# Attention over a cache on one Trainium2 core: transposed scores, unshifted exp and row sums by a ones-matmul, in place of shifted softmax with transposes of P

## The chip, the cores and the metric

The kernel runs on one core of one Trainium2 chip. The metric is the device time of one execution in microseconds (us). Each kernel is run several times; medians are given with the lowest and the highest run. All times that I compare are of runs with a granted TensorE clock near full speed, unless the text says otherwise.

The engines are called as in the profile: PE (TensorE matmul), PEld (TensorE weight load, which overlaps PE), DVE (VectorE), ACT (ScalarE), POOL (GpSimd) and SP (SyncE, which here issues all loads). "SPq" is SP's sequence of DMA issues.

## The reference, cut to what matters

The program does the same attention block twice, for inputs A and B, and puts the two results side by side.

```python
# B, Sq, D = 16, 144, 448;  H, Sk, Dh = 16, 512, 256;  all inputs bf16
q = (x @ wq).reshape(B, Sq, H, Dh)            # -> b h q d
scores = einsum("bhqd,bhkd->bhqk", q, k_cache) * Dh ** -0.5
p = softmax(scores, axis=-1)
o = einsum("bhqk,bhkd->bhqd", p, v_cache)
out = o.reshape(B, Sq, H * Dh) @ wo           # 448 columns; A and B are concatenated
```

A "unit" in this text is one head of one batch of one input: 2 x 16 x 16 = 512 units. Each needs 256 KB of K and 256 KB of V from memory, so K and V together are 268 MB.

## The kernel before

It is a software pipeline. While unit `i` goes through its last product, later units are at earlier stages. Queries lie on the partitions of the score matrix, so 144 queries need a piece of 112 and a remainder of 32. The remainders of four units are packed into one tile. The maximum of each row is taken (DVE), the exponential is shifted by it and sums its row on the way (ACT), P is normalized (POOL), and P is transposed on PE, because the product with V needs keys on the partitions.

```python
def t_load_k(SG):                              # K: one transposing load of 2 MB for 8 units
    src = ks[pr].rearrange("b h k d -> (b h k) d")[r0 * SK:(r0 + 8) * SK, :]     # 512 B rows
    return q.dma_start_transpose(kt_sb[:, sl, :, :], src)...
def t_load_v(G):                               # V: one plain load of 1 MB for 4 units
    src = vs[pr][b, h0:h0 + 4].rearrange("u (p c) d -> p u (c d)", p=128)
    return q.dma_start(v_sb[:, sl, :, :], src)...
def t_sa(U):                                   # scores of 112 queries, 512 keys wide
    for dc in range(2):
        t.matmul(sa_ps[bank][0:QA, :], lhsT=qt_sb[:, U % NQT, dc, 0:QA],
                 rhs=kt_sb[:, ksl, dc, ko:ko + SK], start=(dc == 0), stop=(dc == 1))
def t_exp(U):
    a.activation(pa_sb[0:QA, psl, :], sa_ps[bank][0:QA, :], AF.Exp,
                 bias=stat[0:QA, NEG + sl:NEG + sl + 1], scale=1.0,
                 accum_out=stat[0:QA, RSUM + sl:RSUM + sl + 1])
# ... t_recip: 1/row sum, 112x1, DVE; t_norm: P times 1/row sum, POOL
def t_ta(U):                                   # transposes of P on PE
    src = pa_sb[0:QA, psl, :].rearrange("q (p c) -> q c p", c=4)
    for c in range(4):
        t.transpose(pta_ps[bank][:, c * 128:c * 128 + QA], src[:, c, :], ident[0:QA, 0:QA])
# ... t_sb, t_exp_b, t_norm_b, t_tb: the same for the remainders of four units at once
def t_pv(U):                                   # O transposed, 8 matmuls of 144 columns
    for dc in range(2):
        for c in range(4):
            t.matmul(ot_ps[ob][:, dc * SQ:(dc + 1) * SQ],
                     lhsT=v_sb[:, vsl, j, c * DH + dc * 128:c * DH + (dc + 1) * 128],
                     rhs=pt_sb[:, sl, c, :], start=(c == 0), stop=(c == 3))
# ... the order of the loads: sorted by the unit that needs them first
for SG in range(NSG):
    dl = 8 * SG - LSB
    lo = 8 * (SG - NK) + 7 - LS + 1 if SG >= NK else s_min
    plan(lo, dl, 12, t_load_k, SG)
for G in range(NG):
    dl = 4 * G
    lo = 4 * (G - NV) + 3 + 1 if G >= NV else s_min
    plan(lo, dl, 8, t_load_v, G)
```

All these loads go through one queue, SP's, in the order of the plan. So the queue carries K, V, V, K, V, V and so on: one transposing load for every two plain ones.

## Time and profile before

| | before |
|---|---|
| time, 3 runs | 1215.06 us (1213.36 to 1216.5) |
| first product with V starts at | 37.9 us |
| from one unit's PV to the next | median 2.01, mean 2.278 us |
| after the last PV | 8.3 us |

The first lines of the profile page of the kernel before: span, then busy time of each engine with its share and number of instructions, then the chain of work that ended last, by engine.

```profile
span 1210.9 us, 33868 instructions
...
PE 1176.6 (97%) x13952; PEld 902.6 (75%) x13952; DVE 770.1 (64%) x2179; ACT 753.9 (62%) x2213; POOL 679.6 (56%) x682
...
PE 90%; DMA 6%; DVE 2%; SPq 1%; ACT 0%; issue 0%; POOL 0%; ACTq 0%
```

PE is the bound: 97% busy, and 90% of the chain. (The mean step is above the median because only some steps carry an output projection.)

Groups of instructions of the kernel before: line, engine, operation, tiles, shapes, count, then total busy us, mean ns of one, and the engine's idle time before them with what ended it.

```profile
L418 PE MATMUL sa_ps<-kt_sb,qt_sb 128*112 128x512 bf16 x1024 | 311.1, 385 | 1.0 <-DVE pt_sb L481 0.8
...
L471 PE MATMUL sa_ps<-ident,pa_sb 112*128 112x112 bf16 x2048 | 186.5, 213 | 0.1
...
L450 DVE RECIPROCAL stat<-stat 112x1 f32<-112x1 f32 x512 | 78.4, 153 | 0.5 <-ACT pa_sb L440 0.5
L342 PE MATMUL sb_ps<-kt_sb,qt_sb 128*32 128x512 bf16 x1024 | 67.9, 385 | 10.5 <-DMA kt_sb<-in_A_k_cache_dram 7.9 <-DMA kt_sb<-in_B_k_cache_dram 0.8 <-issue 0.6
```

The change removes the first, the second and the last of these from PE. The third is a reciprocal of one column, 153 ns; the trace has none of more than one column (that of the remainders, 128x1, also takes 153 ns). The mean of one matmul holds its latency; what a matmul costs PE is the distance to the next, which I read from the timeline.

### The profile page before, as it was taken

What the parts mean: (1) busy time and instruction counts of PE and PEld (TensorE: products, weight loads), DVE (VectorE), ACT (ScalarE), POOL (GpSimd) and SP (SyncE); (2) the same over time, 40 slices, a digit from 0 to 9 for tenths busy, and PEclk for the clock granted to TensorE, in tenths of its full rate; (3) what the DMA queues carried; (4) which work ended last, traced back from release to release, by engine and by line L of the source; (5) the groups of instructions that cost most, each with busy time, mean ns of one, the idle gap of its engine ahead of it and who ended that gap; (6) DMA issues with size and microseconds to landing.
All of it is one profiled execution on the core that took longest, in us unless ns stands there. A gap on an engine that the chain in (4) does not pass through costs nothing.

```text
span 1210.9 us, 33868 instructions
## 1 busy us (share of the span) xinstructions
PE 1176.6 (97%) x13952; PEld 902.6 (75%) x13952; DVE 770.1 (64%) x2179; ACT 753.9 (62%) x2213; POOL 679.6 (56%) x682
## 2 busy tenths in 40 slices
PE   4998999999999999999999999999999999999997
PEld 3676777777777777777777777777877777777765
DVE  1765666666666666666566666666666666666563
ACT  1655666666666666666566666666666666666553
POOL 0654565565555565565555655655655655655553
PEclk9999999999999999999999999999999999999999
DMA  9999999999999999999999999999999999999971
GB/s 250 296 269 290 246 255 225 242 251 246 245 238 234 228 263 231 239 239 233 278 284 272 278 272 267 247 257 224 245 245 236 226 245 244 244 239 243 223 178 47
DMA packets 627033, 294.15 MB, mean 243 GB/s; under 512 B 548416, under 2 KB 556608, under 8 KB 626880
## 3 DMA queue, kind: packets, MB, share of 16 engines
q1 hardware_dynamic: 625152, 287.85, 102.2%
q0 software_dynamic: 1728, 4.13, 1.2%
q8 instruction: 111, 1.82, 0.6%
q14 instruction: 42, 0.34, 0.1%
HBM read 148.90 MB, written 4.13 MB: 126 GB/s over the span
## 4 chain that ended last, share of the span: by engine, by line
PE 90%; DMA 6%; DVE 2%; SPq 1%; ACT 0%; issue 0%; POOL 0%; ACTq 0%
PE qp_ps L314 20%; PE ot_ps L504 19%; PE sa_ps L418 18%; PE op_ps L542 17%; PE sa_ps L471 8%; PE sb_ps L342 5%; DMA kt_sb<-in_A_k_cache_dram 4%; PE sb_ps L394 2%; DMA kt_sb<-in_B_k_cache_dram 1%; DVE stat L429 1%; DMA wq_sb<-in_A_wq_dram 0%; PE qp_ps L542 0%; SPq L280 0%; DVE qt_sb L326 0%; DVE pt_sb L481 0%
## 5 line engine op out<-in xcount | busy, mean ns | idle before, releaser
L458 POOL TENSOR_TENSOR pa_sb<-pa_sb,stat 112x512 bf16<-112x512 bf16 x512 | 532.7, 1041 | 491.6 <-DVE stat L450 491.4
L440 ACT ACTIVATE pa_sb<-sa_ps,stat 112x512 bf16<-112x512 f32 x512 | 352.0, 688 | 409.6 <-DVE stat L429 408.6
L429 DVE TENSOR_REDUCE stat<-sa_ps 112x1 f32<-112x512 f32 x512 | 353.9, 691 | 324.7 <-PE sa_ps L418 321.4
L314 PEld LDWEIGHTS qp_ps<-xt_sb,wq_sb 128*128 128x128 bf16 x4096 | 290.5, 99 | 93.1 <-issue 11.3
L314 PE MATMUL qp_ps<-xt_sb,wq_sb 128*128 128x144 bf16 x4096 | 344.1, 228 | 16.1 <-DMA wq_sb<-in_A_wq_dram 10.3
L504 PE MATMUL ot_ps<-pt_sb,v_sb 128*128 128x144 bf16 x4096 | 340.9, 226 | 0.0
L418 PE MATMUL sa_ps<-kt_sb,qt_sb 128*112 128x512 bf16 x1024 | 311.1, 385 | 1.0 <-DVE pt_sb L481 0.8
L542 PE MATMUL op_ps<-wo_sb,ring 128*128 128x448 bf16 x1120 | 279.6, 353 | 0.0
L504 PEld LDWEIGHTS ot_ps<-pt_sb,v_sb 128*128 128x128 bf16 x4096 | 269.1, 98 | 0.4
L471 PEld LDWEIGHTS sa_ps<-ident,pa_sb 112*128 112x128 bf16 x2048 | 161.2, 114 | 104.9 <-ACT pa_sb L440 24.8
L519 ACT ACTIVATE ring<-ot_ps 128x288 bf16<-128x288 f32 (+8 forms) x512 | 190.3, 372 | 4.5 <-PE ot_ps L504 4.5
L481 DVE COPY pt_sb<-sa_ps 128x448 bf16<-128x448 bf16 x512 | 190.5, 372 | 2.4 <-PE sa_ps L471 2.4
L471 PE MATMUL sa_ps<-ident,pa_sb 112*128 112x112 bf16 x2048 | 186.5, 213 | 0.1
L326 DVE TENSOR_SCALAR qt_sb<-qp_ps 128x288 bf16<-128x288 f32 x256 | 117.0, 457 | 98.2 <-PE qp_ps L314 97.5
L382 POOL TENSOR_TENSOR pb_sb<-pb_sb,stat 128x512 bf16<-128x512 bf16 x128 | 133.1, 1040 | 27.1 <-DVE stat L374 27.1
L330 ACT ACTIVATE qt_sb<-qp_ps 128x288 bf16<-128x288 f32 x256 | 106.0, 414 | 35.1 <-PE qp_ps L314 33.4
L418 PEld LDWEIGHTS sa_ps<-kt_sb,qt_sb 128*112 128x112 bf16 x1024 | 96.9, 129 | 38.5 <-issue 26.8
L542 PEld LDWEIGHTS op_ps<-wo_sb,ring 128*128 128x128 bf16 x1120 | 95.5, 98 | 28.1 <-issue 0.9
L440 ACT ACTIVATION_READ_ACCUMULATOR pa_sb<-sa_ps,stat 112x1 f32 x512 | 98.9, 193 | 0.0
L354 DVE TENSOR_REDUCE stat<-sb_ps 128x1 f32<-128x512 f32 x128 | 87.1, 680 | 3.6 <-PE sb_ps L342 3.6
L364 ACT ACTIVATE pb_sb<-sb_ps,stat 128x512 bf16<-128x512 f32 x128 | 88.5, 691 | 0.0
L450 DVE RECIPROCAL stat<-stat 112x1 f32<-112x1 f32 x512 | 78.4, 153 | 0.5 <-ACT pa_sb L440 0.5
(23 smaller groups left out, 368.4 us busy)
## 6 DMA issues: line engine op xcount, KB each, us to landing
v_sb<-in_A_v_cache_dram SPq DMA_DIRECT2D x64, 1024.0 KB, 6.0
v_sb<-in_B_v_cache_dram SPq DMA_DIRECT2D x64, 1024.0 KB, 6.1
out_dram<-ost_sb POOLq DMA_DIRECT2D x36, 112.0 KB, 5.1
wo_sb<-in_A_wo_dram SPq DMA_DIRECT2D x8, 448.0 KB, 7.4
wo_sb<-in_B_wo_dram SPq DMA_DIRECT2D x8, 448.0 KB, 5.7
wq_sb<-in_A_wq_dram SPq DMA_DIRECT2D x4, 768.0 KB, 6.2
wq_sb<-in_B_wq_dram SPq DMA_DIRECT2D x4, 768.0 KB, 7.8
wq_sb<-in_A_wq_dram SPq DMA_DIRECT2D x4, 128.0 KB, 6.6
```

Of the source, the lines that this page charges most:

```text
L314: ins = t.matmul(qp_ps[:, dc * SQ:(dc + 1) * SQ], lhsT=wq_sb[:, kc, c0:c0 + 128], rhs=xt_sb[:, xsl, kc, xo:xo + SQ], start=(kc == 0 and dc ...
L326: return v.tensor_scalar(qt_sb[:, sl, :, :], src, 1.0 / 16.0, None, op0=ALU.mult)
L382: return g.tensor_tensor(pb_sb[:, psl, :], pb_sb[:, psl, :], stat[:, RINVB + sl:RINVB + sl + 1].to_broadcast([128, SK]), op=ALU.mult)
L418: ins = t.matmul(sa_ps[bank][0:QA, :], lhsT=qt_sb[:, U % NQT, dc, 0:QA], rhs=kt_sb[:, ksl, dc, ko:ko + SK], start=(dc == 0), stop=(dc == 1))
L429: return v.tensor_reduce(stat[0:QA, NEG + sl:NEG + sl + 1], sa_ps[bank][0:QA, :], axis=AX.X, op=ALU.max, negate=True)
L440: return a.activation(pa_sb[0:QA, psl, :], sa_ps[bank][0:QA, :], AF.Exp, bias=stat[0:QA, NEG + sl:NEG + sl + 1], scale=1.0, accum_out=stat ...
L458: return g.tensor_tensor(pa_sb[0:QA, psl, :], pa_sb[0:QA, psl, :], stat[0:QA, RINV + sl:RINV + sl + 1].to_broadcast([QA, SK]), op=ALU.mult)
L471: ins = t.transpose(pta_ps[bank][:, c * 128:c * 128 + QA], src[:, c, :], ident[0:QA, 0:QA])
L481: return v.tensor_copy(pt_sb[:, sl, :, 0:QA], pta_ps[bank][:, 0:512].rearrange("p (c q) -> p c q", c=4)[:, :, 0:QA])
L504: ins = t.matmul(ot_ps[ob][:, dc * SQ:(dc + 1) * SQ], lhsT=v_sb[:, vsl, j, c * DH + dc * 128:c * DH + (dc + 1) * 128], rhs=pt_sb[:, sl, c, ...
L519: ins = a.activation(ring[:, 2 * h:2 * h + 2, c0:c0 + n1], src[:, :, 0:n1], AF.Copy)
L542: ins = t.matmul(acc[0:m, 0:D], lhsT=ring[:, c, col0:col0 + m], rhs=wo_sb[:, c, :], start=(c == first), stop=(c == last))
```

## The change

The intent is to take work off PE. With keys on the partitions of the scores (K as weights, Q as moving data) the scores come out already transposed, for all 144 queries at once, so the transposes of P and the whole remainder path go away. Rows of P then lie across partitions, so the maximum and the row sum are no longer cheap on DVE and ACT. The maximum is dropped (exp unshifted, with a check that the sums stayed within 2 to the power of plus or minus 40, else the old kernel runs as a fallback inside the same program). The row sums come from PE: POOL adds the four key chunks in fp32, and one ones-matmul in float32r sums over the partitions and hands every partition the result. The reciprocal is taken of a full 128x144 tile, and the normalization moves to the eviction of O. K is read as rows of 2 KB (four keys) instead of 512 B, so that the scores' key order fits that of V.

The core of the diff, put in order of the functions, with cuts marked; the copy of the old kernel as the fallback, about two thirds of it, is left out.

```diff
-    LQ, LS, LT = 15, 5, 2
-    NK, NV, NXG = 3, 3, 3
+    LQ, LS = 15, 2
+    NK, NV, NXG = 5, 4, 3
 ...
-    kt_sb = sb("kt_sb", [128, NK, 2, 8 * SK], BF16)
+    kt_sb = sb("kt_sb", [128, NK, 8, UG * 128], BF16)        # UG = 4 heads
+    ones = sb("ones", [128, 128], F32R)
+    ps_sb = sb("ps_sb", [128, NPS, SQ], F32R)
 ...
     def t_load_k(G):
-        src = ks[pr].rearrange("b h k d -> (b h k) d")[r0 * SK:(r0 + 8) * SK, :]
+        src = ks[pr].rearrange("b h (p c) d -> (b h p) (c d)", c=4)[r0 * 128:(r0 + UG) * 128, :]
         return q.dma_start_transpose(kt_sb[:, sl, :, :], src)...
 ...
+    def t_s(U):                       # 8 matmuls of 144 columns
+        for c in range(4):
+            for dc in range(2):
+                t.matmul(s_ps[bank][:, c // 2, (c % 2) * SQ:(c % 2 + 1) * SQ],
+                         lhsT=kt_sb[:, ksl, 2 * c + dc, jj * 128:(jj + 1) * 128],
+                         rhs=qt_sb[:, U % NQT, dc, :], start=(dc == 0), stop=(dc == 1))
+    def t_presum(U):                  # POOL
+        g.tensor_tensor(pp_sb[:, sl, :, :], pt_sb[:, psl, 0:2, :], pt_sb[:, psl, 2:4, :], op=ALU.add)
+        g.tensor_tensor(ps_sb[:, sl, :], pp_sb[:, sl, 0, :], pp_sb[:, sl, 1, :], op=ALU.add)
+    def t_sum(U):                     # PE
+        t.matmul(ot_ps[ob][:, 2 * SQ:3 * SQ], lhsT=ones[:, :], rhs=ps_sb[:, sl, :], start=True, stop=True)
+    def t_recip(U):                   # DVE, 128x144
+        v.reciprocal(rinv_sb[:, sl, :], ot_ps[ob][:, 2 * SQ:3 * SQ])
+    def t_check(U):                   # DVE, twice per unit
+        for k, op in ((0, ALU.max), (1, ALU.min)):
+            v.tensor_tensor(run_sb[:, k, :], run_sb[:, k, :], rinv_sb[:, sl, :], op=op)
 ...
-        for SG in range(NSG):
-            dl = 8 * SG - LSB
-            plan(lo, dl, 12, t_load_k, SG)
+        for G in range(NG):
+            dl = UG * G - LS
+            lo = UG * (G - NK) + UG - 1 - LS + 1 if G >= NK else s_min
+            plan(lo, dl, 20, t_load_k, G)
```

## The prediction

> **What bounds it now.** TensorE. Busy shares (part 1): PE 97%, DVE 64%, ACT 62%, POOL 56%; the chain that ended last is 90% PE, 6% DMA. In the timeline around 600 us the PE is back to back: Q 0.50 us per unit (8 matmuls, 62 ns apart), scores 0.44, transposes of P 0.19, PV 0.51, output projection 0.185 per matmul (0.405 per unit), 32-row remainder 0.13 and its transposes 0.055. Sum 2.23 us x 512 units = 1142 us (K loads repeat every 18.0 us per 8 units: 2.25). The rest is start (first PV at 37.9 us), tail (8 us after the last PV) and early waits for K (waits view: 8.7 us).
>
> DMA is second. It looks 90% busy, but by packets it has slack: K transposes run at 290 GB/s (18 ns per 256 B packet), V at 390 to 400; 7.3 us for 2 MB of K plus 2 x 2.7 us for V plus 1.5 to 2.5 us of switching is about 15 us of the 18. Estimated DMA floor: 970 us.
>
> **What changes on PE, per unit.** Out: scores 0.44, remainder scores 0.13, transposes 0.19 + 0.055 = 0.82 us. In: 8 score matmuls of 128x144, like PV, 0.51 us; one float32r ones-matmul, x. So T = 0.50 + 0.51 + 0.51 + 0.405 + x = 1.92 + x, against 2.23. The trace has no float32r matmul. The Trainium skill, "FP8 and Floating Point Precision", TensorE Precision Notes, describes reduced-precision FP32 as one 4-byte read truncated, against four passes for true FP32. One pass is 0.06 us; I add about 0.11 us for a weight load that is not hidden: x = 0.17, possible 0.06 to 0.40. T = 2.09 us. All of it is critical.
>
> **Other engines, per unit (estimates from this trace).** ACT: exp over 576 columns about 0.70, Q eviction 0.41: 1.15 us. POOL: 288- and 144-element adds at 1041 ns per 512: about 0.9 us (now 1.3). DVE: reciprocal of 144 columns about 0.31 (one per column plus the 0.153 us of one element), scaled eviction of 288 columns 0.46, two running max/min about 0.25 each: 1.3 us. None exceeds T. Exp and adds take about 2 us of the 4 before the sum needs them.
>
> K from 2 KB rows moves the same bytes in the same 256 B pieces; I expect it neutral, within 10% of 290 GB/s. The check costs 2 to 4 us at the end.
>
> **Sum.** 512 x 2.09 = 1070, + start and tail about 42, + 5 of stalls and check: about **1118 us**, 8% less. Range 1058 to 1215. Chances: faster 0.80, same 0.10, slower 0.10.
>
> **Signs.** Right: PE still over 93% of the span and of the chain; the score, Q and PV groups 62 to 64 ns apart; sum matmul adding 0.1 to 0.25 us to the step; POOL and DVE below 75%; eight-unit period near 16.7 us.
>
> **What would make it wrong.** (1) The skill's "VectorE: DVE Perf Modes" (slices) gives reciprocal a repeat count of 8; one element here (0.153 us) can't tell. At 8 cycles per column it costs about 1.36 us, DVE then needs 2.3 to 2.5 us per unit and bounds the kernel at 1190 to 1290. (2) Slower K transposes from 2 KB strides, or more switching stalls: PE waits on K. (3) DVE and POOL slowing each other.

## More of the kernel before

The DMA queue of the kernel before in its middle, from the timeline of SP: start, length until the next issue is possible, instruction.

```profile
432.98 3.72 SPq L299 DMA_DIRECT2D v_sb<-in_A_v_cache_dram  x2
436.75 12.05 SPq L290 DMA_TRANSPOSE kt_sb<-in_A_k_cache_dram  x1
448.85 5.66 SPq L299 DMA_DIRECT2D v_sb<-in_A_v_cache_dram  x2
454.55 13.43 SPq L290 DMA_TRANSPOSE kt_sb<-in_A_k_cache_dram  x1
```

And what the queue itself waited for in the kernel before, in total us, times, longest:

```profile
SPq L299 <- PE op_ps L542: 235.3, 59, 12.8
SPq L299 <- PE ot_ps L504: 40.1, 15, 8.0
```

The queue waits some 275 us for PE to free the buffers of V. So the DMA is faster than the kernel needs, but not by 275 us: during most of these waits an earlier load is still on its way. By the landings in the trace, this queue was without a load in flight for only about 16 us before its last landing at 1185 us.

## The result, and the profile after

| | before | after |
|---|---|---|
| time, 4 runs each, same rounds | 1214.21 us (1212.06 to 1216.5) | 1172.11 us (1169.79 to 1177.78) |
| ratio of fast runs, 95% interval | | 0.9662 (0.9632 to 0.9691) |
| first PV starts at | 37.9 us | 36.9 us |
| PV to PV, median / mean | 2.01 / 2.278 us | 2.01 / 2.198 us |
| after the last PV | 8.3 us | 15.3 us |

Ratios in this text are the mean time of one kernel's fast runs over the mean of the other's of the same rounds, so they are not quite the ratio of the medians quoted. The change gained 42 us, against the 96 us that were forecast. The time lies inside the forecast range, but less than half of the gain came.

The same three lines of the page, after:

```profile
span 1176.0 us, 32740 instructions
...
PE 1087.5 (92%) x13952; PEld 961.7 (82%) x13952; DVE 1009.5 (86%) x2184; ACT 560.1 (48%) x1061; POOL 645.1 (55%) x1065
...
PE 64%; DMA 21%; DVE 8%; SPq 4%; issue 1%; ACT 1%; POOL 0%; POOLq 0%; ACTq 0%
```

PE is busy 89 us less (1176.6 to 1087.5); the forecast was 72 (512 x 0.14). But its share of the chain fell from 90% to 64%, and DMA with SPq has 25%, DVE 8%. Two new limits have taken part of the gain.

Groups after:

```profile
L1035 DVE RECIPROCAL rinv_sb<-ot_ps 128x144 f32<-128x144 f32 x512 | 540.4, 1055 | 136.5 <-PE ot_ps L1025 129.5
L988 POOL TENSOR_TENSOR pp_sb<-pt_sb 128x288 f32<-128x288 bf16 x512 | 374.9, 732 | 474.5 <-ACT pt_sb L979 472.4
...
L967 PE MATMUL s_ps<-qt_sb,kt_sb 128*128 128x144 bf16 x4096 | 343.1, 227 | 33.9 <-DMA kt_sb<-in_A_k_cache_dram 18.6 <-DMA kt_sb<-in_B_k_cache_dram 15.1
...
L1063 DVE TENSOR_TENSOR run_sb<-run_sb,rinv_sb 128x144 f32<-128x144 f32 x1024 | 276.6, 311 | 0.0
...
L1025 PE MATMUL ot_ps<-ps_sb,ones 128*128 128x144 f32 x512 | 161.1, 315 | 0.0
L1025 PEld LDWEIGHTS ot_ps<-ps_sb,ones 128*128 128x128 f32 x512 | 98.2, 192 | 0.0
```

The reciprocal takes 1055 ns, not the 310 of the prediction. The two check operations take 311 ns each. The ones-matmul needs a weight load of 192 ns, where a bf16 weight load takes 98. On the score line, PE sits idle 33.9 us in total until K lands.

What PE waited for after, in us, times, longest (the DMA lines of the view of waits):

```profile
PE s_ps L967 <- DMA kt_sb<-in_A_k_cache_dram: 18.6, 19, 2.4
PE s_ps L967 <- DMA kt_sb<-in_B_k_cache_dram: 15.1, 11, 3.4
...
PE qp_ps L939 <- DMA wq_sb<-in_B_wq_dram: 6.6, 3, 4.9
...
PE qp_ps L939 <- DMA xt_sb<-in_A_x_dram: 4.0, 2, 2.1
PE op_ps L1098 <- DMA wo_sb<-in_B_wo_dram: 3.8, 2, 3.5
...
PE ot_ps L1013 <- DMA v_sb<-in_A_v_cache_dram: 1.9, 3, 0.8
```

With 1.5 us more for x of the second input, these sum to 51.5 us. Before, everything but the first load was 8.7 us, shown above on L342. It isn't only K: whatever comes through that queue is late.

The queue after, in the same window as before:

```profile
437.12 0.58 SPq L924 DMA_DIRECT2D v_sb<-in_A_v_cache_dram  x1
437.75 6.84 SPq L915 DMA_TRANSPOSE kt_sb<-in_A_k_cache_dram  x1
444.63 0.58 SPq L924 DMA_DIRECT2D v_sb<-in_A_v_cache_dram  x1
445.26 7.15 SPq L915 DMA_TRANSPOSE kt_sb<-in_A_k_cache_dram  x1
452.45 0.58 SPq L924 DMA_DIRECT2D v_sb<-in_A_v_cache_dram  x1
```

And the largest waits of V's issues for PE:

```profile
SPq L924 <- PE qp_ps L939: 17.0, 39, 1.1
SPq L924 <- PE s_ps L967: 16.6, 27, 1.5
```

Before, the queue waited 235 us and 40 us for a free V buffer in its two largest lines. Now the largest are 17 us each, none longer than 1.5 us. All waits of V's issues for PE are 59 us now, in 117 pieces, and K and V alternate without a pause in the window shown. By the landings in the trace, the queue had a load in flight all the time from its first issue to its last landing at 1146.5 us, with gaps of under 1 us in all. The DMA's slack is gone, and it is the DMA that sets the pace over long stretches. What the queue moved is on the page: packets, MB, and the time of the packets as a share of 16 engines' span (packets overlap, so it can exceed 100%).

```profile
q1 hardware_dynamic: 627200, 287.86, 109.1%
```

K and V are 268 MB of it. The other 19 MB are x and the weights, which go through the same queue.

The waits cost a little more than their length. This is PE's timeline after the longest wait for K: start, us, instructions, and in brackets the idle time before.

```profile
600.27 0.68 PE L967 MATMUL s_ps<-qt_sb,kt_sb 128*128 128x144 bf16 x8 [3.45 <-DMA kt_sb<-in_B_k_cache_dram]
...
601.59 1.18 PE L939 MATMUL qp_ps<-xt_sb,wq_sb 128*128 128x144 bf16 x8
...
604.66 0.67 PE L939 MATMUL qp_ps<-xt_sb,wq_sb 128*128 128x144 bf16 x8
```

After 3.45 us of idleness the eight Q matmuls that start 1.3 us later take 1.18 us, and the next eight, at 604.66, 0.67 again. The Trainium skill, "TensorE: Matmul & The Clock Gate", What's actually happening, says that the clock halves after an idle window of about 3.4 us and comes back after about the same time of work; here the trace's record of the clock agrees: it is halved from 601.18 to 604.60 us. Less idleness was enough elsewhere: the clock is halved at 720.65 us after an idle stretch of 2.1 us, and in the kernel before at 586.74 us after one of 2.0 us. All slowed matmuls together cost about 7 us by my count (outside start and end the clock was halved for 27 us), and the mean granted clock fell from 0.997 to 0.985.

### The profile page after: what moved, and what is told of

Its sections match the earlier page's. It is cut to its first block, busy times and chain, and to the rows that moved or that the text cites. A ratio compares the mean times of both kernels' runs of the same rounds, so it can differ in the third digit from the quotient of the medians.

```text
span 1176.0 us, 32740 instructions
## 1 busy us (share of the span) xinstructions
PE 1087.5 (92%) x13952; PEld 961.7 (82%) x13952; DVE 1009.5 (86%) x2184; ACT 560.1 (48%) x1061; POOL 645.1 (55%) x1065
## 4 chain that ended last, share of the span: by engine, by line
PE 64%; DMA 21%; DVE 8%; SPq 4%; issue 1%; ACT 1%; POOL 0%; POOLq 0%; ACTq 0%
PE qp_ps L939 16%; PE s_ps L967 15%; PE ot_ps L1013 15%; PE op_ps L1098 15%; DMA kt_sb<-in_B_k_cache_dram 9%; DMA kt_sb<-in_A_k_cache_dram 8%; DVE rinv_sb L1035 4%; PE ot_ps L1025 3%; SPq L905 2%; DVE run_sb L1063 2%; DVE ring L1050 2%; DMA v_sb<-in_A_v_cache_dram 1%; DMA xt_sb<-in_A_x_dram 1%; SPq L915 1%; SPq L906 1%; DMA wq_sb<-in_A_wq_dram 1%
## 5 line engine op out<-in xcount | busy, mean ns | idle before, releaser
L1035 DVE RECIPROCAL rinv_sb<-ot_ps 128x144 f32<-128x144 f32 x512 | 540.4, 1055 | 136.5 <-PE ot_ps L1025 129.5
L988 POOL TENSOR_TENSOR pp_sb<-pt_sb 128x288 f32<-128x288 bf16 x512 | 374.9, 732 | 474.5 <-ACT pt_sb L979 472.4
L955 ACT ACTIVATE qt_sb<-qp_ps 128x288 bf16<-128x288 f32 x512 | 210.0, 410 | 470.4 <-PE qp_ps L939 470.3
L979 ACT ACTIVATE pt_sb<-s_ps 128x576 bf16<-128x576 f32 x512 | 332.9, 650 | 108.9 <-PE s_ps L967 67.8
L967 PE MATMUL s_ps<-qt_sb,kt_sb 128*128 128x144 bf16 x4096 | 343.1, 227 | 33.9 <-DMA kt_sb<-in_A_k_cache_dram 18.6
L967 PEld LDWEIGHTS s_ps<-qt_sb,kt_sb 128*128 128x128 bf16 x4096 | 275.4, 98 | 42.6 <-DMA kt_sb<-in_A_k_cache_dram 22.5
L1063 DVE TENSOR_TENSOR run_sb<-run_sb,rinv_sb 128x144 f32<-128x144 f32 x1024 | 276.6, 311 | 0.0
L992 POOL TENSOR_TENSOR ps_sb<-pp_sb 128x144 fp32r<-128x144 f32 x512 | 251.7, 492 | 40.1
L1050 DVE TENSOR_TENSOR ring<-ot_ps,rinv_sb 128x288 bf16<-128x288 f32 (+8 forms) x640 | 242.4, 395 | 17.7
L1025 PE MATMUL ot_ps<-ps_sb,ones 128*128 128x144 f32 x512 | 161.1, 315 | 0.0
```

The source lines that it names most:

```text
L955: return a.activation(qt_sb[:, sl, :, :], src, AF.Copy)
L967: ins = t.matmul(s_ps[bank][:, c // 2, (c % 2) * SQ:(c % 2 + 1) * SQ], lhsT=kt_sb[:, ksl, 2 * c + dc, jj * 128:(jj + 1) * 128], rhs=qt_sb[ ...
L979: return a.activation(pt_sb[:, psl, :, :].rearrange("p (a b) q -> p a (b q)", a=2), s_ps[bank][:, :, 0:2 * SQ], AF.Exp, scale=DH ** -0.5)
L988: return g.tensor_tensor(pp_sb[:, sl, :, :], pt_sb[:, psl, 0:2, :], pt_sb[:, psl, 2:4, :], op=ALU.add)
L992: return g.tensor_tensor(ps_sb[:, sl, :], pp_sb[:, sl, 0, :], pp_sb[:, sl, 1, :], op=ALU.add)
L1025: return t.matmul(ot_ps[ob][:, 2 * SQ:3 * SQ], lhsT=ones[:, :], rhs=ps_sb[:, sl, :], start=True, stop=True)
```

## The experiments

I held two theories of where the missing 54 us (1172 less 1118) went, and a third way of reading the first:

- **Supply.** The DMA can't bring K and V as fast as PE now uses them. My first version of it (A1 where the texts say so) blamed the number of switches between K and V in the queue: K and V alternate one to one now, where before there was one K for two V. Another version blames the 2 KB rows, and a third the number of transposing loads.
- **DVE.** The reciprocal is slower than forecast; DVE, 86% busy, holds buffers that PE needs.
- **PE itself.** The steps of the prediction's sum, above all the ones-matmul, may have been too small.

Every kernel of one batch ran on one chip beside the kernel before (medians of that: 1212.7 to 1214.2).

### Taking DVE's and the DMA's load away: nocheck, halfk, halfk_nocheck

`nocheck` drops the two check operations of each unit (only the reduction at the end stays, over an untouched tile).

```diff
                 t_evac_ot(u)
-                t_check(u)
```

> After, without the running max/min of the reciprocals per unit (DVE falls from 1.97 to about 1.43 us per unit; result still right, but unguarded). Theory A, the supply of K through the DMA queue bounds the kernel: 1155 to 1175 us, no gain beyond 1.5%. Theory B, DVE at 1.97 us per unit bounds it: 1095 to 1120 us.

`halfk` loads K only for every second group of four units, and the group between uses its neighbour's. It computes a wrong thing; it shows the kernel with half of the K traffic. `halfk_nocheck` does both.

```diff
-            ksl = G % NK
+            ksl = (G - G % 2) % NK
 ...
-            plan(lo, dl, 20, t_load_k, G)
+            if G % 2 == 0:
+                plan(lo, dl, 20, t_load_k, G)
```

> After, loading only every second K group and using it twice (wrong result on purpose): a quarter of the DMA bytes gone, every instruction of PE, DVE, ACT and POOL kept. Theory A: 1085 to 1115 us, PE over 95% busy, no waits for K. Theory B (DVE): 1150 to 1175 us.

> Both at once (wrong result on purpose): what PE alone allows. Dense step from the trace of after: 24 matmuls at 63 ns, 0.119 us for the sum, 0.405 us of output projection = 2.04 us x 512 + 42 = about 1087 us. Theory A: within 1.5% of halfk. Theory B: far below halfk.

| kernel | us, 4 runs | ratio to before |
|---|---|---|
| after | 1172.11 (1169.79 to 1177.78) | 0.966 |
| nocheck | 1162.29 (1159.23 to 1169.11) | 0.9565 (0.9536 to 0.9594) |
| halfk | 1110.79 (1110.52 to 1112.39) | 0.9154 (0.9133 to 0.9174) |
| halfk_nocheck | 1094.82 (1094.68 to 1095.33) | 0.9019 (0.900 to 0.9038) |

The busy lines of `halfk`, then of `halfk_nocheck`:

```profile
PE 1071.7 (97%) x13952; PEld 954.4 (86%) x13952; DVE 1006.5 (91%) x2184; ACT 560.0 (51%) x1061; POOL 645.2 (58%) x1065
```

```profile
PE 1063.8 (97%) x13952; PEld 954.7 (87%) x13952; DVE 786.6 (72%) x1160; ACT 560.0 (51%) x1061; POOL 641.7 (59%) x1065
```

This divides the time. With both loads lightened PE is 97% busy at 1095 us, and no DMA wait but the first one is left in `halfk`. Putting the check back costs 16 us (1110.8 less 1094.8). Putting the other half of K back costs 61 us more (1172.1 less 1110.8). Of those 61, the waits listed above are 51.5 and the slowed matmuls about 7. So the main loss is supply, the smaller one DVE, and PE alone does what the prediction's sum says, as shown further down. (`halfk` also has half of K's loads and half of the changes between K and V in the queue, so it shows that supply costs 61 us, not what in the supply does.)

A caution that holds for all K edits here: `halfk` was compared with the reference and found correct, though half of its K is wrong. The comparison passes with these inputs, so "correct" is weak evidence that a K layout is right. For `kold` and `k8` below I have only the agreement of the indices in the code besides.

### Is it the rows, or the order in the queue? kold and pair

`kold` reads K from 512 B rows as the kernel before did, in the same groups of four units, with a strided weight access to match.

```diff
-            src = ks[pr].rearrange("b h (p c) d -> (b h p) (c d)", c=4)[r0 * 128:(r0 + UG) * 128, :]
+            src = ks[pr].rearrange("b h k d -> (b h k) d")[r0 * SK:(r0 + UG) * SK, :]
 ...
-                                       lhsT=kt_sb[:, ksl, 2 * c + dc, jj * 128:(jj + 1) * 128],
+                                       lhsT=kt_sb[:, ksl, dc, jj * SK:(jj + 1) * SK].rearrange("d (p c) -> d c p", c=4)[:, c, :],
```

> After, with K transposed from 512 B rows as in the kernel before (1 MB loads kept; the weights of the score matmuls are then read with a stride of 4). Theory A1, the switches between transposes and plain loads cost, not the row size: 1160 to 1185 us, K packets at the same 18 ns. Theory A2, the 2 KB rows slow the transposes: 1150 us or less. Theory A3, the 2 KB rows help them: 1195 us or more.

It took 1176.67 us (1168.63 to 1185.03), ratio 0.9687 (0.9624 to 0.9749), the same as after. The times from issue to landing of K's loads, by the view of that line, are also the same; first after, then `kold`:

```profile
DMA to landing us min/median/max: 7.1/10.6/15.1
```

```profile
DMA to landing us min/median/max: 6.9/10.7/14.6
```

In both, and in the kernel before, K moves at about 290 GB/s while it moves alone, and a packet of 256 B takes 18 ns. The Trainium skill, "DMA: Bandwidth & Descriptors", Latency and other measured facts, gives 261 GB/s for transposing loads with a non-contiguous middle dimension and 350 to 400 for contiguous ones; this case shows 290 for 512 B and for 2 KB rows alike. The prediction's "neutral" was right about rows.

`pair` keeps everything but the order: K, K, V, V instead of K, V, K, V.

```diff
-            dl = UG * G - LS
-            lo = UG * (G - NK) + UG - 1 - LS + 1 if G >= NK else s_min
+            dl = UG * (G - G % 2) - LS
+            G1 = G - G % 2 + 1
+            lo = UG * (G1 - NK) + UG - 1 - LS + 1 if G1 >= NK else s_min
 ...  # and V likewise
```

> After, with the loads issued two K groups, then two V groups, instead of one and one: same bytes, same buffers, half as many switches between transposes and plain loads. Theory A with about 1 us lost per switch (249 us lost in 238 switches of the trace of after): 1100 to 1140 us. Theory B (DVE): no change, 1165 to 1180 us. If the deeper wait for two free buffers costs more than the switches: slower than 1180.

It took 1142.72 us (1137.93 to 1148.59), ratio 0.9428 (0.9392 to 0.9465): 29 us gained with the same loads, and PE waits no more for K. Its largest wait for K or V in `pair` is now one for V:

```profile
PE ot_ps L1013 <- DMA v_sb<-in_B_v_cache_dram: 6.6, 2, 3.3
```

At this point I took the switches between K and V for the cause.

### The ladder on top of pair: pair_x_v5, pair_x_v5_pck, pair_x_v5_pck_bf, pair_pck

I tried to build on that. `pair_x_v5` adds a fifth V buffer (one x buffer less) and loads x 16 units earlier. `pck` moves half of the check to POOL: a running sum of the reciprocals in place of their maximum (a sum of positive numbers is at least their maximum, so the check stays safe). `bf` makes the ones and the partial sums bf16, so that the ones-matmul is a bf16 one. `pair_pck` is `pair` with that check alone. (The two `pair_x_v5` kernels with `pck` also get a third buffer for the reciprocals, `pair_pck` doesn't.)

```diff
-    NK, NV, NXG = 5, 4, 3
+    NK, NV, NXG = 5, 5, 2
 ...
-            dl = u_first - LQ
+            dl = u_first - LQ - (16 if XG else 0)
 ...  # pck
-            for k, op in ((0, ALU.max), (1, ALU.min)):
+            for k, op in ((0, ALU.add), (1, ALU.min)):
-                S.add(DVE, e, ...
+                S.add(DVE if k else POOL, e, ...
 ...  # bf
-        ones = sb("ones", [128, 128], F32R)
+        ones = sb("ones", [128, 128], BF16)
-        ps_sb = sb("ps_sb", [128, NPS, SQ], F32R)
+        ps_sb = sb("ps_sb", [128, NPS, SQ], BF16)
```

> The paired order, with five V groups instead of four (room from one x buffer less) and x asked for 16 units earlier. The trace of pair has four waits of 3 to 4 us for V and x and about 6 us of matmuls at the lower clock after them: without them 1115 to 1128 us. If what is left in pair is something else (DVE, raw DMA rate): 1138 us or more.

> The same, with the upper half of the check as a running sum on GpSimd (one add of 144, about 0.49 us, instead of a running max on DVE). DVE falls from 1.97 to 1.71 us per unit, GpSimd rises from 1.26 to 1.75. halfk against halfk_nocheck says that DVE is worth at most 16 us: 1100 to 1118 us.

> The same, with the presums written in bf16 and a bf16 ones-matmul in place of float32r. The sum adds 0.119 us to the step of PE in the trace of after; at bf16 it should add 0.063: 0.056 x 512 = 29 us less if PE bounds, 1072 to 1092 us. If DMA or DVE bounds by then: less than 10 us gained.

> The paired order with the upper half of the check as a sum on GpSimd, nothing else: the plain candidate for a better kernel. 1130 to 1143 us: DVE relief is worth 0 to 12 us beside DMA.

| kernel | us | ratio to before |
|---|---|---|
| pair | 1142.72 (1137.93 to 1148.59) | 0.9428 |
| pair_pck | 1142.97 (1141.58 to 1145.81) | 0.9413 |
| pair_x_v5 | 1141.61 (1139.65 to 1144.96) | 0.9404 |
| pair_x_v5_pck | 1138.65 (1136.81 to 1140.57) | 0.9385 |
| pair_x_v5_pck_bf | 1135.87 (1130.83 to 1141.97) | 0.9343 |

All of it together gains 7 us; the gains expected of `pair_x_v5` and of `pck`, 24 us and more, didn't come. In the last of these PE still waits 32 us for V, where `pair` had 9. Work taken from PE and DVE comes back as waiting, as it must where the DMA sets the pace. The bf16 step did shorten PE's own step: the ones-matmul adds 62 ns instead of 119, and the median step falls from 2.009 to 1.941 us.

### Switches, or transposing loads? split_same and split_alt

`split_same` cuts each load of K into two of two heads, issued back to back. The number of switches between K and V doesn't change; the number of transposing loads of K doubles to 256. `split_alt` cuts V as well and alternates the halves, so that both double.

```diff
-        def t_load_k(G):
+        def t_load_k(G, part):
-            src = ...[r0 * 128:(r0 + UG) * 128, :]
+            r1 = (r0 + 2 * part) * 128
+            src = ...[r1:r1 + 256, :]
 ...
-            plan(lo, dl, 20, t_load_k, G)
+            for part in range(2):
+                plan(lo, dl, 20, t_load_k, G, part)              # split_same
+                plan(lo, dl + 2 * part, 20 + 2 * part, t_load_k, G, part)   # split_alt, and V likewise
```

> After, each 1 MB load of K as two transposes of 2 heads issued one behind the other, V unchanged: twice the transposes, the same 256 switches. Theory A1 (the switch costs): 1165 to 1185 us. Rival A5 (each transpose instruction or smaller piece costs): 128 more at about 0.65 us each, 1225 to 1265 us.

> After, K in halves and V in halves, taking turns (K V K V per group of 4 heads): twice the switches, about 512. The traces put a switch at about 0.65 us of lost DMA time: if DMA bounds, up to 166 us more, 1260 to 1340 us under A1. If the gain of pair came from anything but the number of switches: within 2% of after.

`split_same` took 1268.67 us (1260.22 to 1271.87), ratio 1.0464 (1.044 to 1.0487). `split_alt` took 1261.12 us (1258.45 to 1268.34), ratio 1.0396 (1.0353 to 1.044). The largest DMA waits of PE in `split_same`, then in `split_alt`, where the deadlines of the halves shift the waiting from K to V:

```profile
PE s_ps L969 <- DMA kt_sb<-in_A_k_cache_dram: 54.1, 42, 2.9
...
PE s_ps L969 <- DMA kt_sb<-in_B_k_cache_dram: 43.8, 40, 3.9
```

```profile
PE ot_ps L1017 <- DMA v_sb<-in_A_v_cache_dram: 60.5, 27, 8.8
...
PE ot_ps L1017 <- DMA v_sb<-in_B_v_cache_dram: 38.9, 24, 4.0
```

The switches can't be the only cost. Without one switch more, the time rose by 96 us, slightly above what A5 expected and far above A1; with twice the switches, it rose no further (its 1261 us lie just inside A1's range, but A1 can't explain `split_same`). So cutting K's loads in two costs by itself: (1268.7 less 1172.1) / 128 = 0.755 us for each transposing load added, in a queue that is the bottleneck. `pair` stands against the opposite reading, that switches cost nothing: it gained 29 us with the same loads.

### Fewer transposing loads: k8

`k8` undoes the part of the change that the prediction didn't price: it loads K for eight units at a time, as the kernel before, but keeps the 2 KB rows. Two more things change with it. The order of the queue becomes K, V, V again, with half of the switches, as in `pair`. And three such buffers replace five small ones (24 units of K instead of 20), and x, Q and the output get fewer buffers so that all fits; no run tests these alone.

```diff
-    NK, NV, NXG = 5, 4, 3
+    NK, NV, NXG = 3, 4, 2
-        kt_sb = sb("kt_sb", [128, NK, 8, UG * 128], BF16)
+        kt_sb = sb("kt_sb", [128, NK, 8, 8 * 128], BF16)
 ...
-            src = ...[r0 * 128:(r0 + UG) * 128, :]
+            src = ...[r0 * 128:(r0 + 8) * 128, :]
-        for G in range(NG):
-            dl = UG * G - LS
+        for G in range(NT // 8):
+            dl = 8 * G - LS
```

> After, with K loaded as one 2 MB transpose per 8 heads (three such buffers; room from one x buffer, three Q slots and one output slot), V unchanged, result right: 64 transposes of K instead of 128. Theory A5 (each transpose instruction costs about 0.75 us of DMA time, from split_same): 48 us less DMA need, so the kernel comes near the floor of halfk (1111): 1112 to 1132 us, waits for K under 15 us. Theory A1 (switches only): like pair, 1135 to 1145.

It took 1126.5 us (1124.51 to 1129.66), ratio 0.9283 (0.926 to 0.9305): 46 us less than after and 16 less than `pair`, inside A5's range and below A1's. The K waits of PE and the queue in `k8`:

```profile
PE s_ps L967 <- DMA kt_sb<-in_B_k_cache_dram: 5.1, 3, 2.7
...
PE s_ps L967 <- DMA kt_sb<-in_A_k_cache_dram: 3.8, 2, 2.1
```

```profile
439.21 14.91 SPq L915 DMA_TRANSPOSE kt_sb<-in_A_k_cache_dram  x1
454.17 1.12 SPq L924 DMA_DIRECT2D v_sb<-in_A_v_cache_dram  x2
455.34 15.46 SPq L915 DMA_TRANSPOSE kt_sb<-in_A_k_cache_dram  x1
```

PE waits 8.9 us for K instead of 33.7; before the change it was 8.7. So the halving of K's loads, with the order of the queue that comes with it, costs 46 us. That is 0.71 us for each of the 64 loads, close to the 0.755 of `split_same`, but the two can't be set side by side: `k8` also has half of the switches of after, and being only 16 us above `halfk` it is in part bound by PE and DVE.

The landings in the traces show the queue itself. The queue time below counts each load from the later of its issue and the landing before it, to its own landing, summed over all loads of the profiled run. In all five kernels a load was in flight up to the last landing, with gaps of under 1 us in all.

| kernel | order for eight units | transposing loads of K | switches, about | queue time, us | that run, us |
|---|---|---|---|---|---|
| k8 | K V V | 64 | 128 | 1083 | 1125.8 |
| pair | K K V V | 128 | 128 | 1097 | 1137.9 |
| after | K V K V | 128 | 256 | 1146 | 1177.8 |
| split_same | K K V K K V | 256 | 256 | 1238 | 1263.3 |
| split_alt | K V K V K V K V | 256 | 512 | 1233 | 1260.7 |

From `k8` to `pair`, 64 more loads at equal switches add 13 us; from `pair` to after, 128 more switches at equal loads add 49; from after to `split_same`, 128 more loads at equal switches add 92; doubling both adds 87. No single price for a load, or for a switch, gives all four. What is shown is that the same bytes cost more in smaller pieces and in an order that alternates.

### Other suspects: wide, vact, vact_bf, vact_pck_bf

The traces also hold 111 instruction fetches of 16 KB, each about 1.05 us long on one DMA engine. In stretches with K alone, all engines' transposes lose about 1.5 us around one (mean of 24 cases after, 30 before, by my own reading of the packets). `wide` has fewer instructions: Q, scores and PV as 4 matmuls of 288 columns each instead of 8 of 144. Its result is wrong (relative error 0.95).

```diff
-                    for dc in range(2):
-                        ins = t.matmul(qp_ps[:, dc * SQ:(dc + 1) * SQ], ...
+                    ins = t.matmul(qp_ps[:, 0:2 * SQ], lhsT=wq_sb[:, kc, h * DH:h * DH + 128],
+                                   rhs=xt_sb[:, xsl, kc, x2:x2 + 2 * SQ], ...
 ...  # scores and PV likewise
```

> After, with Q, scores and PV as 4 matmuls of 288 columns in place of 8 of 144 (wrong result on purpose, same columns, same DMA issues, 12,288 fewer instructions of PE). In the traces the 16 KB instruction fetches cost the K transposes about 1.5 us each (111 of them). Theory A4, these stalls are a large part of what DMA loses: fetches fall to about 63, PE's step by only 0.03 us, time 1090 to 1125 us. If fetches don't matter (only switches do): 1155 to 1172.

It took 1148.56 us (1138.78 to 1151.32), ratio 0.9434 (0.939 to 0.9478), and missed what both theories expected. The queue line of instruction fetches (packets, MB, share), after and then in `wide`:

```profile
q8 instruction: 111, 1.82, 0.6%
```

```profile
q8 instruction: 63, 1.03, 0.4%
```

Of 48 fetches less, 24 us came. Half a microsecond each would fit, but PE's median step also fell, by 0.08 us and not by the 0.03 expected (2.010 to 1.931; 40 us over 512 units if PE alone bounded), so the fetches' share stays open. They can't explain the difference between before and after, which have 111 each.

`vact` issues the loads of V from ACT, on a second queue beside K.

```diff
-            S.add(SP, e, writes=[(("v", sl), G)], dma_sem="v%d" % sl, name="v%d" % G)
+            S.add(ACT, e, writes=[(("v", sl), G)], dma_sem="v%d" % sl, name="v%d" % G)
 ...
-            lo = UG * (G - NV) + UG - 1 + 1 if G >= NV else s_min
+            lo = UG * (G - NV) + UG - 1 + 3 if G >= NV else s_min
```

> After, with the V loads issued from ACT (their own queue, 3 units after the buffer is free at the soonest), everything else as in after, result right. If switching within one queue and V standing behind K is what costs: V and K mix, 1105 to 1135 us. If the DMA engines themselves are full: 1160 to 1180 us. If ACT is held up by its waits: slower than 1180.

> vact with the bf16 presum and ones-matmul. If DMA no longer bounds vact, up to 29 us less than vact where PE bounds, about 10 to 15 where DVE (1.97 us per unit) does; if DMA still bounds, within 5 us of vact.

> The same with half of the check on GpSimd as a sum (DVE 1.71 us per unit). If PE bounds: step 1.98 us, 1065 to 1085 us. If DMA bounds: within 5 us of vact_bf.

`vact` took 1281.46 to 1288.93 us in its three fast runs (a fourth, of 1348.05, was slow), ratio of the fast runs 1.0587 (1.0548 to 1.0625): worse by some 112 us, and uneven. `vact_bf` ran from 1260.79 to 1440.27 us, with two of four runs slow and no ratio; `vact_pck_bf`, which also has a third buffer for the reciprocals, took 1271.23 to 1282.91 us in three fast runs, ratio 1.0498 (1.0464 to 1.0533), and up to 1339.79 in three slow ones. Its profile fell in a slow run, so I read nothing from it. The landing times of K in `vact`, to set against those of after shown above:

```profile
DMA to landing us min/median/max: 6.9/12.8/43.6
```

A load of K now needed up to 43.6 us, and PE waited 124 us for K. In a stretch from about 450 to 610 us all DMA together moved only 104 to 168 GB/s. One expectation for more than 1180 us was that ACT would be held up by its waits; but PE waited only 7.9 us for V, which ACT issues, so what was late is K. Here the waits between the two kinds of load in one queue are cheaper than mixing them; why K slows down so much isn't shown.

### Putting it together: k8_pck_bf and k8_bf

`k8_pck_bf` is `k8` with half of the check on POOL and the bf16 ones-matmul; `k8_bf` leaves the check on DVE.

> The same with the bf16 sum and half of the check on GpSimd. If DMA is off the critical path in k8: PE's step 1.98 and DVE at 1.71 us, 1075 to 1100 us. If DMA still bounds: within 8 us of k8.

> k8 with the bf16 sum alone, the check left on DVE. In the trace of k8_pck_bf the one check left on DVE took 521 ns where two took 2 x 311 in after, so moving the other to GpSimd freed almost nothing: 1110 to 1120 us, within 6 us of k8_pck_bf. If moving it did help: 1122 us or more.

`k8_pck_bf` took 1115.58 us (1113.14 to 1117.81), ratio 0.9181 (0.9164 to 0.9197): the fastest of all whose result was found right, 8% faster than the kernel before and 5% faster than after. I had expected 1075 to 1100. `k8_bf` took 1119.82 us (1117.27 to 1125.51), ratio 0.9239 (0.9204 to 0.9275), 4 us more. By these medians the bf16 sum gives 7 us and the moved check 4, by the ratios about 5 and 7; for the sum alone the intervals of the ratios overlap. Clear of the noise are only the two together, 11 us. That `k8_bf` stayed below 1122 fits the expectation that moving the check freed little. The check's two halves in `k8_pck_bf`, in the groups:

```profile
L1063 DVE TENSOR_TENSOR run_sb<-run_sb,rinv_sb 128x144 f32<-128x144 f32 x512 | 267.0, 521 | 0.0
L1063 POOL TENSOR_TENSOR run_sb<-run_sb,rinv_sb 128x144 f32<-128x144 f32 x512 | 257.3, 502 | 5.1 <-DVE rinv_sb L1035 5.1
```

After, DVE did both operations in 276.6 us. Now it does one, and is busy 267.0 us with it: one operation takes 521 ns instead of 311. Both engines read the same two kinds of tile at the same time, and DVE gained nothing. The Trainium skill, "GPSIMD Engine Reference", 1. Specifications, says that GpSimd shares its SBUF interfaces with VectorE and names instructions with two SBUF inputs as a case of contention; these lines agree, with 521 against 311 ns. And PE's waits for K rose again, from 8.9 us in `k8` to 27.9: a faster PE is met by the same DMA.

## Why the prediction was right or wrong

**Right: PE's own time.** The step was 1.92 + x. Of x, the prediction had 0.17; the trace shows that the ones-matmul starts 28 ns after the last PV matmul and the next group 154 ns after it, where matmuls of 144 columns normally follow at 63, so x = 28 + 154 - 63 = 119 ns. With that the prediction's own sum is 512 x 2.039 + 47 = 1091 us, and `halfk_nocheck`, with DMA and DVE relieved, took 1095, with a mean step of 2.039 us in its trace. What the Trainium skill, "FP8 and Floating Point Precision", TensorE Precision Notes, says of a truncated fp32 read against four passes fits: four passes of 144 columns would take, by estimate, at least 4 x 63 = 252 ns, and 119 were added.

**Wrong, and decisive: "DMA is second", with an "Estimated DMA floor: 970 us".** The step that failed is this floor: about 15 us of DMA for eight units, "7.3 us for 2 MB of K plus 2 x 2.7 us for V plus 1.5 to 2.5 us of switching". The queue of after was never empty and took 1146 us to its last landing, while PE's own time with start and tail is 1091. The queue times above split the difference of 176 us:

- 64 x 15 is 960, so the floor leaves 10 us for x and the weights. Their 19 MB take 85 us of the queue in after, 75 more.
- Even with K in pieces of 2 MB, as before the change, K and V took 15.7 us for eight units (`k8`), 45 us more over the 64. So the old pieces need up to 1083 us, and not 970: about as much as PE. (Up to, because in `k8`, too, some issues of V waited briefly for a free buffer.)
- With K in pieces of 1 MB, which the change brings and the prediction doesn't mention, it was 16.6 us, 56 us more. In kernel time this part is the 46 us of `k8`, of the 61 us that supply costs in all.

That K "moves the same bytes in the same 256 B pieces; I expect it neutral" was right as far as it went: the bytes, the pieces, the 290 GB/s and the row size are as forecast. The size of one load and the order of the queue are what it left out. The allowance of 1.5 to 2.5 us of switching had been read off the kernel before and carried over to a queue with another mix of loads. Risk (2) of the prediction named this outcome, "PE waits on K", and gave two reasons: 2 KB strides, which `kold` rules out, and "more switching stalls", of which `pair` shows 29 us; but it put no price on them in the sum.

**Wrong, smaller: "DVE: reciprocal of 144 columns about 0.31".** It took 1.055 us. With the one-column reciprocal of 0.153 us, that is by estimate (1055 - 153) / 143 = 6.3 ns per column (if the fixed part is the same: the one reads SBUF, the other PSUM), or six cycles at the 0.96 GHz that the Trainium skill, "VectorE: DVE Perf Modes", Specifications, gives for VectorE. The slices walkthrough of that page speaks of a repeat count of 8, from which the prediction's risk (1) estimated 1.36 us with that clock; six cycles lie between this and the one of its sum. DVE was busy 1009.5 / 512 = 1.97 us per unit instead of 1.3, just below PE's step. It doesn't bound the kernel on average, but it holds the bank that PE wants next: PE waited for DVE in small pieces (PV's weight loads sat idle 11.0 us in total for the eviction of O), and the check behind the reciprocal costs 16 us where the DMA doesn't hide it (`halfk` against `halfk_nocheck`) and 10 where it does (`nocheck`). The check had been put at 2 to 4 us at the end only. The end did grow, too: 15.3 us after the last PV instead of 8.3.

**Also off, without effect:** POOL was forecast at 0.9 us per unit and the two adds take 732 + 492 ns = 1.22. ACT was forecast at 1.15 and takes 650 + 410 ns = 1.06.

So the account closes: 1118 of the prediction, less 26 for the smaller x (512 x 0.051), is 1092; PE alone was measured at 1095; with 16 for DVE and 61 for supply it is 1172. Only the first step is a test, 1092 against 1095; the 16 and the 61 are differences of the runs and add up by themselves. That 1172 lies in the range of 1058 to 1215 is luck: by the prediction's own sum x alone, from 0.06 to 0.40 us, spans 1061 to 1235, and the range wasn't made for a queue at its limit.

**The signs.** Failed: PE over 93% of span and chain (92% and 64%), DVE below 75% (86%), eight-unit period near 16.7 us (8 x 2.198 = 17.6). Held: matmuls of 144 columns about 63 ns apart, the sum adding 0.1 to 0.25 us (0.119), POOL below 75% (55%).

**What stays open.** Smaller loads of K and more switches cost queue time, each shown by a pair of runs at which the other stays the same (`split_same`, `pair`). How the two share the 46 us of `k8` isn't shown: 16 us are its lead over `pair`, which has the same number of switches, and PE and DVE hide part of that. A count of all borders between loads of which at least one transposes explains `pair`, but would give `split_alt` about twice the rise that was measured. At such borders the packets show 0.3 to 1.0 us with little moving (the median of each kind; under 100 GB/s), and none between two loads of V in `pair` and `k8`; I don't know what the hardware does in it. How much the instruction fetches cost is open as well.

## What to carry to other kernels

When a change speeds up the bottleneck, price the second resource at the new pace with its own pieces: count its instructions, their sizes and their order before and after, not only the bytes, because here halving the transposing loads, with the order that came of it, cost 46 us at the same bytes. Count everything that the resource carries, too: 19 MB of x and weights took 85 us of the queue. And waits of a queue aren't its slack while earlier loads are in flight. A cost known for one element doesn't price an instruction of 144, so leave such a term wide in the sum and not only in the list of risks. And when the chain shows a new limit, take one load away at a time (`halfk`, `nocheck`): two runs told more than any reading of the waits, and the repair (`k8`) gave back most of the loss by undoing the unpriced part.

## What the Trainium skill lacked or had wrong

- "DMA: Bandwidth & Descriptors" gives no cost in queue time for cutting transposing loads into smaller ones or for alternating them with plain loads. Here, at equal bytes and in a queue that was the bottleneck, 128 more loads of K at the same switches added 96 us (0.755 each), and half of the switches at the same loads took off 29. Its two rates for transposing loads, 261 and 350 to 400 GB/s, don't fit either: 290 GB/s for 512 B and for 2 KB rows, while K moves alone.
- The same page doesn't give the cost of plain loads on a second queue beside transposing loads: about 1285 us instead of 1172, with K landing after up to 43.6 us instead of 15.1.
- "TensorE: Matmul & The Clock Gate" has the clock halve after an idle window of about 3.4 us; here idle stretches of 2.0 and 2.1 us were enough.
- "VectorE: DVE Perf Modes" gives no time for reciprocal, and its repeat count of 8 isn't the cost per column: 128x144 took 1055 ns, by estimate 6.3 ns per column, about 6 cycles.
- "FP8 and Floating Point Precision" gives no time for float32r, and "TensorE: Matmul & The Clock Gate", Weight-path perf modes, excludes fp32 weights from its fast weight load, while the page has one time for weight loads whatever their type: 192 ns for 128x128 float32r weights against 98 ns in bf16, and 119 ns added by one 144-column matmul against 62.
- "GPSIMD Engine Reference" names the shared interfaces but no size of the effect (the skill's page on SBUF goes further into the sharing): a DVE operation with two fp32 inputs of 128x144 took 521 ns beside a like one on POOL, 311 where DVE did both halves of the check.
- The page on the runtime tells of instruction fetches in blocks of 16 KB, but no page that I read says what they cost other DMA: 111 fetches in 1176 us, with about 1.5 us lost by transposing loads around one, by my reading of 24 cases.
